# Attention, channel mixing and expert layer in one kernel: PSUM banks shared across two stages, mixing products placed inside the second products, and the conversion of the third weights started a chunk later

## The chip, the core and the metric

The kernel runs as one program on one of the eight cores of a Trainium2 chip. The metric is the device time of one execution in microseconds (us). The core's engines run side by side, each with a queue that it takes in order: TensorE (PE, matrix products into PSUM; PEld is its weight load), VectorE (DVE), ScalarE (ACT), GpSimd (POOL) and SyncE (SP, which here only issues DMAs). PSUM has eight banks of 128 x 512 fp32; a matrix product writes into one bank, and a bank is used again only after its last reader.

## The reference

```python
scores = scale * q @ k.T + bias          # 2 batches, 8 heads, 768 x 768, head dim 64; 8 global and 96 local keys kept
x = softmax(scores) @ v                  # -> x (2, 768, 512)
u = x + (x^T @ U @ V)^T                  # mixing over the sequence, rank 32
x = u + relu(u @ w_ch1) @ w_ch2          # channel sums, hidden 2048
logits = x @ w_gate; local_gate = sigmoid(x @ w_local)
e = argmax(logits) where s == 0 or local_gate < 0.5, else the e of the token before
out = p[e] * (relu(x @ w1[e]) @ w2[e])   # 8 experts, hidden 1024
```

Inputs are fp32, except U, V, w_ch1 and w_ch2, which come as 64-bit floats and are converted on the chip.

## The kernel before, in words

The order of work on each engine is written out by hand: the program order of the instructions is the order of each queue, and generators stepped between other work place the small pieces. A product of two fp32 operands is three products of halves (`three`: high x high, high x low, low x high); a high half is a copy by ACT, the low half a subtraction by DVE or POOL that reads it.

*Attention* runs over 16 heads and 6 tiles of 128 rows. Between its steps the first conversions of weights go along: `load_w1` issues the loads of 64-bit weights on SP, and `from_f64` (lines 217 to 224) turns a piece of 128 x 512 into fp32 with one ACT and four DVE instructions. `load_pair` and `load_v` put the heads' inputs on the same SP queue.

*Channel sums.* `chunks(b, ...)` goes over 16 chunks of 128 hidden channels, batch 0 and then batch 1. In each, `gemm1` makes two halves of 384 tokens, each 12 products into a bank g of two; ACT and DVE make hh and hl of them. `gemm2` of the chunk before then goes over six token tiles, three products each, into the six sums y. Beside it run: `convert(p + 2)`, one step per half and per tile (16 steps, then a load of the weights after next); `split_w1` (`prep`), which gives high halves to ACT and low halves to POOL (line 244, two pieces per pair of chunks); and a `Weave`, ticked once per half and per tile, which for batch 0 steps `mixing(1)`. That sums t1 over six tiles of batch 1 (line 483; its high and low parts come from lines 489 and 487), waits MXW ticks, and then makes six products mx (line 499) into banks of g, each added to x by DVE (line 500), MXS ticks apart. After the chunks, the last few `gemm2` go tile by tile, and `tail` adds each finished sum to x (line 647), stores it (line 648, on SP), and for batch 1 hands it to `routing`, stepped by `late` inside what follows: transposes xt, logits lp (line 717), the choice on DVE (lines 723 to 767), sums over tokens (ab, line 754), slots (sl, line 771), and lists written by POOL.

*PSUM.* In this stage the pool psc holds six banks acc (t1 of batch 1 and the sums y), and psg two for everything else (g). At the end of batch 1 psc is closed, and pools psz (four acc, the experts' sums z) and pss (two side tiles, for `late`) are opened over the same banks.

*Experts.* Two fillers of 128 tokens (positions -2 and -1) come first, while the router finishes; then eight positions of one or two tiles. `unit` takes two chunks of hidden channels of an expert. With one tile it makes egr, which ACT turns into eh (line 1208); the next unit transposes it (`turn_`, etr; hh by ACT on line 1216, hl by DVE on line 1217), and `out_` makes the six products into z. `after` ticks `late` and steps the splits of coming expert weights (line 834 on ACT, line 837 on DVE). `filler_load` issues those weights on SP (line 817).

Of the kernel before, what the change touches and what calls it, by code (L numbers as in the profile page):

```python
# [9 lines left out]
F32 = mybir.dt.float32  # L10
# [9 lines left out]
PSUM = bass.MemoryType.PSUM  # L20
DRAM = bass.MemoryType.DRAM

P = 128
# [6 lines left out]
NP1 = FC1 // 2  # L30
FC2 = 8
NP2 = FC2 // 2
# [37 lines left out]
def tile_kernel(ctx, tc, q, k, v, nn, U, V, w12, wg, wgt, ew, masks, lst0, out, dbg=None):  # L70
    nc = tc.nc
# [10 lines left out]
    def g_tile(name):  # L82
        return g_pool[-1].tile([P, 512], F32, tag="g", name=name)
# [7 lines left out]
    def drain(gen):  # L91
        while gen is not None and run(gen):
            pass
# [152 lines left out]
    def convert(p):  # L246
        w_f[p] = wf0_tile(f"wf{p}") if p < 2 else wf_tile(f"wf{p}")
        for c in range(2):
            raw = w_raw.pop((p, c))
            for h in (0, 512):  # L250
                yield from from_f64(w_f[p][:, c, h:h + 512], sq_w, raw[:, h:h + 512])
            if p + 1 < NP1:
                load_w1(p + 1, c)
# [216 lines left out]
    def mixing(b):  # L470

        if b == 0:
            ut_tiles(0)
            parts = [[t.rearrange("p k c -> p (k c)")[:, DM * i:DM * i + DM] for t in ut[0]] for i in range(NT)]
        else:
            parts = [[mix_room[i % 2][:, w, DM * (i // 2 % 2):DM * (i // 2 % 2) + DM] for w in range(2)] for i in range(NT)]
        t1 = (g_tile if b == 0 else acc_tile)(f"t1_{b}")
        lag = LAGM[b]
        for i in range(NT + lag):
            j = i - lag  # L480
            if j >= 0:
                for w in range(2):
                    nc.tensor.matmul(
                        t1, u_sb[:, j].rearrange("p a r -> p (a r)"), parts[j][w], start=(j == 0 and w == 0), stop=(j == NT - 1 and w == 1))
            if 0 < i <= NT:
                hi, lo = parts[i - 1]
                (nc.gpsimd if (i - 1) % 4 in LOP[b] else nc.vector).tensor_tensor(lo, x_t[b, i - 1], hi.bitcast(F32), ALU.subtract)
            if i < NT:
                nc.scalar.copy(parts[i][0], x_t[b, i])
            yield  # L490
        tm = utp.tile([P, DM], F32R, tag="tm", name=f"tm_{b}")
        nc.scalar.copy(tm, t1)
        yield
        nc.vector.tensor_tensor(tm[32:64], t1[32:64], tm[32:64].bitcast(F32), ALU.subtract)
        for _ in range(MXW if b else 1):
            yield
        for i in range(NT):
            mx = g_tile(f"mx{b}{i}")
            nc.tensor.matmul(mx, vst[:, P * i:P * i + P], tm, start=True, stop=True)
            nc.vector.tensor_tensor(x_t[b, i], mx, x_t[b, i], ALU.add)  # L500
            for _ in range(MXS if b else 1):
                yield
# [25 lines left out]
    for z in range(total + LAGV):  # L528
        if z < total:
            n, i = steps[z]  # L530
            zz = z % (2 * NT)
            if zz == LAGV and n // 2 + 1 < len(heads) // 2:
                load_v(n // 2 + 1)
            if n == 2 and i == 0:
                load_w1(0, 0)
                load_w1(0, 1)
            if i == 1 and 0 < n + 1 < H:
                head_bias(n + 1)
            if zz == 1 and n > 1 and n // 2 + 1 < len(heads) // 2:
                load_pair(n // 2 + 1)  # L540
            s = scores(z)
        if z >= LAGT and z - LAGT < total:
            transposed(z - LAGT)
        if z < total:
            softmax(z, s)
        if z == 0:
            other_columns()
        if z >= LAGV:
            values(z - LAGV)
        if z == 2 * NT:  # L550
            flagi = banded_form()
        if z == half - 1:
            banded.append(nc.values_load(flagi[0:1, 0:1], min_val=0, max_val=1))
        if z == half + LAGV:
            drain(mixc)
            t_ctx.close()
            other_windows(0)
            if "x" in dbg:
                for i_ in range(NT):
                    nc.sync.dma_start(dbg['x'][0, P * i_:P * i_ + P, :], x_t[0, i_])  # L560
            utp = u_ctx.enter_context(tc.tile_pool(name="ut", bufs=1, side="right"))
            fill = [mixing(0), transposes(0)]
        if z > half + LAGV and z % FILL[1] < FILL[0] and fill and not run(fill[0]):
            fill.pop(0)
        if z == MZ:
            run(mixc)
        if z > SM0:
            run(small)
        if z > BG0:
            if z % 8 < BGR and bg and not run(bg[0]):  # L570
                bg.pop(0)
# [13 lines left out]
    sm = ctx.enter_context(tc.tile_pool(name="small", bufs=2))  # L585
    m_ctx = ExitStack()
    mp = m_ctx.enter_context(tc.tile_pool(name="moe1", bufs=3))
    c_ctx = ExitStack()
    psc = [c_ctx.enter_context(tc.tile_pool(name="psc", bufs=1, space=PSUM))]

    def acc_tile(name):
        return psc[0].tile([P, 512], F32, tag="acc", bufs=6 if len(psc) == 1 else 4, name=name)

    def side_tile(name):

        return g_tile(name) if len(psc) == 1 else psc[1].tile([P, 512], F32, tag="side", bufs=2, name=name)

    def three(out_, ah, al, bh, bl, start, stop):
        nc.tensor.matmul(out_, ah, bh, start=start, stop=False)
        nc.tensor.matmul(out_, ah, bl, start=False, stop=False)  # L600
        nc.tensor.matmul(out_, al, bh, start=False, stop=stop)  # L601
# [347 lines left out]
    acc = {}  # L949
# [11 lines left out]
    def chunks(b, weave, hook, tail):  # L961

        conv, prep = None, None
        for m in range(FC1):
            p = m // 2
            if m % 2 == 0:
                drain(prep)
                prep = None
                if b == 0 and p + 2 < NP1:
                    drain(conv)  # L970
                    conv = convert(p + 2)
            hook(m)
            if m == 0 or m != 1 and m % 2 == 1 - b:
                if p + 1 < NP1:
                    prep = split_w1(b, p + 1)
                elif b == 0:
                    drain(conv)
                    prep = split_w1(1, 0)
            for _ in gemm1(b, m):
                run(prep, 1)  # L980
                run(conv, 1)
                if b == 1:
                    split_step(2)
                weave.tick()
                if b == 0 and m < 2:
                    weave.tick()
            if m == 0:
                acc[b] = []
            elif m <= FC1 - DEFER[b]:
                for i in range(NT):  # L990
                    if m == 1:
                        acc[b].append(acc_tile(f"y{b}{i}"))
                    gemm2(b, m - 1, i, acc[b])
                    run(conv, 1)
                    if b == 1 and i % 2:
                        split_step()
                    weave.tick()
        weave.finish()
        if prep is not None:
            drain(prep)  # L1000
        hook(FC1)
        for i in range(NT):
            for m in range(FC1 - DEFER[b], FC1):
                gemm2(b, m, i, acc[b])
                if b == 1:
                    late.tick()
            tail(i)
# [52 lines left out]
    chunks(1, wv, fillers_ahead, tail1)  # L1060
    while splits:
        split_until(99)
    c_ctx.close()
    psc[:] = [ctx.enter_context(tc.tile_pool(name=n, bufs=1, space=PSUM)) for n in ("psz", "pss")]
    filler_load(0, 1)
    filler_load(0, 3)

# [106 lines left out]
    def after(step):  # L1174
        late.tick()
        if step:
            split_step()
# [17 lines left out]
    def unit(pos, p, key, xh, xl, n, acc_):  # L1195

        wh, wl = e_hl[key, p]
        if n == 1:
            g = g_tile(f"eg{key}{p}")
            gv = g[:, :256].rearrange("p (a c) -> p a c", a=2)  # L1200
            for kk in range(KC):
                s_ = slice(P * kk, P * kk + P)
# [6 lines left out]
            hh = ep.tile([P, 256], F32R, tag="ehh", bufs=3, name=f"ehh{key}{p}")  # L1209
            hl = ep.tile([P, 256], F32R, tag="ehl", bufs=3, name=f"ehl{key}{p}")  # L1210
# [6 lines left out]
                nc.vector.tensor_tensor(hl, tr[:, :256], hh.bitcast(F32), ALU.subtract)  # L1217

            def out_():
                for c in range(2):  # L1220
                    s_ = slice(P * c, P * c + P)
                    f = 2 * p + c
                    three(acc_[0], hh[:, s_], hl[:, s_], wh[:, c, 512:], wl[:, c, 512:], f == 0, f == FC2 - 1)
                    after("cd"[c] in PACE[pos])
                if p == NP2 - 1:
                    done(pos)

# [11 lines left out]
        else:  # L1239
            for c in range(2):  # L1240
                f = 2 * p + c
# [3 lines left out]
                hh, hl = e_gemm1(key, f, WIDTHS[pos], xh, xl, turn, [end[0][:, w, 256 * (f % 4):256 * (f % 4) + 256] for w in range(2)] if late_f else None)  # L1245
# [92 lines left out]
_OUTS = [((NTOK, DM), "float32")]  # L1338


MXW, MXS = 26, 4
DEFER = (3, 4)
LAGM = 3, 3
SPM = 12, 13, 14
# [101 lines left out]
```

## Time and profile before

| | us |
|---|---|
| three runs | 611.58, 614.37, 614.12 (median 614.12) |
| the profiled execution | 612.27, its span 610.4, mean granted clock 0.989 |
| PE busy | 585.3 (96%) |
| DVE busy | 415.6 (68%) |
| ACT busy | 292.7 (48%) |
| POOL busy | 127.3 (21%) |

The span goes from the first instruction to the last, and the run's time is a little longer. Busy PE counts the modelled time of products that overlap, so PE's gaps and the granted clock say more than its share. Attention takes the span to about 114 us, the chunks of batch 0 to about 252, those of batch 1 to about 411, and fillers and experts the rest. Times in the rows below are in us from the span's start; the arrow in a bracket names what ended the idle time.

### The profile page before, as it was taken

To read this page: it belongs to the slowest core of one execution; us is meant where nothing else is said; L and a number is where in the kernel's file an instruction comes from. 1 tells how busy PE (TensorE), PEld (TensorE's weight loads), DVE (VectorE), ACT (ScalarE), POOL (GpSimd) and SP (SyncE) were. 2 spreads that over 40 slices of the span, in tenths; PEclk is the share of its full clock that TensorE was granted. 3 is DMA by queue.
4 is the path that set the end of the run, shared out by engine and by line. 5 is a ranking of instruction groups with operands and counts; after the bars stand their busy time and mean duration, and the time that the engine had idled before them with its cause. 6 is when DMAs were issued, how large, how long until landed. Compare 5 with 4: busy or idle time off the path is not lost. (4 is left out here: it accounts for less than half of the span.)

```text
span 610.4 us, 9735 instructions
## 1 busy us (share of the span) xinstructions
PE 585.3 (96%) x3469; PEld 519.3 (85%) x3469; DVE 415.6 (68%) x998; ACT 292.7 (48%) x631; POOL 127.3 (21%) x119
## 2 busy tenths in 40 slices
PE   8999999889989999999998999998899999999994
PEld 5998899879878999899997889877788988989893
DVE  5779986498888881348999446566724577685850
ACT  4878877534413432332222116324524677584841
POOL 5010030112213333333330211012230313031101
PEclk9999999899999999999999999997999999999998
DMA  8956651014414300251000038035096578868400
GB/s 215 310 153 202 209 171 49 2 45 162 139 69 139 111 27 1 90 187 35 35 18 0 1 62 319 35 121 155 20 319 247 178 272 319 267 247 319 168 15 35
DMA packets 35850, 83.47 MB, mean 137 GB/s; under 512 B 5631, under 2 KB 17791, under 8 KB 33744
## 3 DMA queue, kind: packets, MB, share of 16 engines
q1 hardware_dynamic: 31632, 70.87, 35.1%
q0 software_dynamic: 2784, 7.62, 3.5%
q10 hardware_dynamic: 1376, 4.26, 1.8%
q8 instruction: 29, 0.48, 0.4%
q14 instruction: 29, 0.24, 0.1%
HBM read 74.34 MB, written 8.77 MB: 136 GB/s over the span
## 5 line engine op out<-in xcount | busy, mean ns | idle before, releaser
L604 ACT ACTIVATE hh<-g 128x384 fp32r<-128x384 f32 x62 | 30.4, 490 | 112.0 <-PE g L601 111.6
L605 DVE SCALAR_TENSOR_TENSOR hl<-g,hh 128x384 fp32r<-128x384 f32 x62 | 34.4, 556 | 52.3 <-ACT hh L604 52.1
L338 PE MATMUL s<-kt,q 128*128 128x232 f32 (+1 forms) x192 | 55.2, 370 | 2.6 <-DVE m L348 1.7
L352 ACT ACTIVATE e<-t,m 128x232 f32<-128x232 f32 (+1 forms) x96 | 45.7, 477 | 17.2 <-DVE m L348 16.7
L672 DVE CUSTOM_DVE_ANT_0 sq_w<-x,wgt 128x512 f32<-128x512 f32 x54 | 47.1, 872 | 1.4
L348 DVE CUSTOM_DVE_ANT_0 t<-s,bias 128x232 f32<-128x232 f32 (+1 forms) x96 | 35.9, 377 | 16.6 <-PE s L338 6.8
L217 ACT ACTIVATE sq_w<-w 128x512 f32<-128x512 f32 x32 | 21.5, 671 | 49.6 <-DVE wf L224 49.6
L859 POOL DMA_INDIRECT out_dram<-x,ids x13 | 13.2, 1013 | 120.6 <-ACT x L858 100.0
L365 ACT COPY et<-pt 128x256 f32<-128x256 f32 (+1 forms) x96 | 33.5, 349 | 6.7 <-PE pt L362 4.7
L362 PE MATMUL pt<-ident,e 128*128 128x128 f32 x176 | 35.0, 273 | 0.0
L338 PEld LDWEIGHTS s<-kt,q 128*128 128x128 f32 x192 | 29.7, 191 | 5.9 <-DVE m L348 3.9
L222 DVE SCALAR_TENSOR_TENSOR wf<-w,wf 128x512 int32<-128x512 int32 x32 | 32.5, 1017 | 0.8
L382 PE MATMUL o<-v,et 128*128 128x65 f32 x160 | 30.9, 275 | 0.0
L780 POOL DMA_INDIRECT lst<-tab,slot x12 | 12.7, 1054 | 81.0 <-DVE tab L776 80.0
L605 DVE SCALAR_TENSOR_TENSOR ehlr<-egr,ehhr 128x192 fp32r<-128x192 f32 (+1 forms) x28 | 10.6, 377 | 26.1 <-ACT ehhr L604 26.1
L220 DVE SCALAR_TENSOR_TENSOR wf<-w,wf 128x512 int32<-128x512 int32 x32 | 27.1, 848 | 1.1 <-DVEq L463 0.7
L362 PEld LDWEIGHTS pt<-ident,e 128*128 128x128 f32 x176 | 24.1, 142 | 4.3 <-ACT et L365 0.5
L381 PE MATMUL o<-v,et 104*128 104x65 f32 x160 | 26.9, 249 | 0.0
L381 PEld LDWEIGHTS o<-v,et 104*128 104x128 f32 x160 | 24.2, 191 | 0.8
L382 PEld LDWEIGHTS o<-v,et 128*128 128x128 f32 x160 | 24.3, 191 | 0.0
L604 ACT ACTIVATE ehhr<-egr 128x192 fp32r<-128x192 f32 (+1 forms) x28 | 9.7, 347 | 29.1 <-PE egr L601 27.6
L224 DVE SCALAR_TENSOR_TENSOR wf<-sq_w,wf 128x512 f32<-128x512 f32 x32 | 22.0, 688 | 1.3
(753 smaller groups left out, 1943.5 us busy)
## 6 DMA issues: line engine op xcount, KB each, us to landing
ew<-in_ew_dram SPq DMA_DIRECT2D x32, 1024.0 KB, 6.8
w<-in_w_dram SPq DMA_DIRECT2D x16, 1024.0 KB, 4.9
v<-in_v_dram SPq DMA_DIRECT2D x8, 704.0 KB, 5.1
ew<-in_ew_dram ACTq DMA_DIRECT2D x4, 1024.0 KB, 12.9
x2d<-x SPq DMA_DIRECT2D x12, 256.0 KB, 2.0
kt<-in_k_dram SPq DMA_DIRECT2D x7, 408.0 KB, 4.5
q<-in_q_dram SPq DMA_DIRECT2D x14, 192.0 KB, 5.5
wgt<-in_wgt_dram SPq DMA_DIRECT2D x4, 512.0 KB, 4.8
```

Of the source, the lines that this page charges most:

```text
L220: nc.vector.scalar_tensor_tensor(t, low, 29, t, ALU.logical_shift_right, ALU.bitwise_or)
L222: nc.vector.scalar_tensor_tensor(t, high, -0x40000000, t, ALU.bitwise_and, ALU.bitwise_or)
L338: nc.tensor.matmul(s[:, :w], qs[n % 2][:, c], kt[:, kc], start=True, stop=True)
L348: nc.vector.tensor_tensor_reduce(out=t[:, :w], in0=s[:, :w], in1=bias[:, h, b0:b0 + w], scale=-0.125, scalar=3.0e38, op0=ALU.add, op1=ALU. ...
L352: nc.scalar.activation(e[:, :w], t[:, :w], AF.Exp, bias=m, scale=-1.0)
L362: nc.tensor.transpose(pt[:, P * j:P * j + P], e[:, c0:c0 + P], ident)
L365: nc.scalar.copy(et[:, :w], pt[:, :w])
L381: nc.tensor.matmul(oo, et[0:REST, 0:P], vt[0:REST, NT + i - 1, vc], start=True, stop=False)
L382: nc.tensor.matmul(oo, et[:, P:256], vt[:, i, vc], start=False, stop=True)
L604: nc.scalar.activation(hi, src, AF.Relu)
L605: nc.vector.scalar_tensor_tensor(lo, src, 0.0, hi.bitcast(F32), ALU.max, ALU.subtract)
L672: nc.vector.tensor_tensor_reduce(out=sq_w, in0=x_t[0, i], in1=rooms[k % 2][:, DM * j:DM * j + DM], scale=1.0, scalar=0.0, op0=ALU.mult, op ...
```

## The change

The pool psc stays open to the end, with four banks acc and two banks side. t1 of batch 1 and the last two sums of each batch use side, the first four acc; the experts' sums go on in acc, and the side tiles of `late` in side, after `beside` is set. `convert(p + 2)` is drained and started at odd chunks and no longer at even ones. MXW and MXS become 31 and 8. In `out_` with one tile, the products that read hl come behind the four others. `load_w1(0, ...)` is called two steps later in attention.

```diff
--- before.py
+++ after.py
@@ -474,7 +474,7 @@
             parts = [[t.rearrange("p k c -> p (k c)")[:, DM * i:DM * i + DM] for t in ut[0]] for i in range(NT)]
         else:
             parts = [[mix_room[i % 2][:, w, DM * (i // 2 % 2):DM * (i // 2 % 2) + DM] for w in range(2)] for i in range(NT)]
-        t1 = (g_tile if b == 0 else acc_tile)(f"t1_{b}")
+        t1 = (g_tile if b == 0 else two_tile)(f"t1_{b}")
         lag = LAGM[b]
         for i in range(NT + lag):
             j = i - lag
@@ -531,7 +531,7 @@
             zz = z % (2 * NT)
             if zz == LAGV and n // 2 + 1 < len(heads) // 2:
                 load_v(n // 2 + 1)
-            if n == 2 and i == 0:
+            if n == 2 and i == 2:
                 load_w1(0, 0)
                 load_w1(0, 1)
             if i == 1 and 0 < n + 1 < H:
@@ -585,15 +585,18 @@
     sm = ctx.enter_context(tc.tile_pool(name="small", bufs=2))
     m_ctx = ExitStack()
     mp = m_ctx.enter_context(tc.tile_pool(name="moe1", bufs=3))
-    c_ctx = ExitStack()
-    psc = [c_ctx.enter_context(tc.tile_pool(name="psc", bufs=1, space=PSUM))]
+    psc = ctx.enter_context(tc.tile_pool(name="psc", bufs=1, space=PSUM))
+    beside = []
 
     def acc_tile(name):
-        return psc[0].tile([P, 512], F32, tag="acc", bufs=6 if len(psc) == 1 else 4, name=name)
+        return psc.tile([P, 512], F32, tag="acc", bufs=4, name=name)
+
+    def two_tile(name):
+
+        return psc.tile([P, 512], F32, tag="side", bufs=2, name=name)
 
     def side_tile(name):
-
-        return g_tile(name) if len(psc) == 1 else psc[1].tile([P, 512], F32, tag="side", bufs=2, name=name)
+        return (two_tile if beside else g_tile)(name)
 
     def three(out_, ah, al, bh, bl, start, stop):
         nc.tensor.matmul(out_, ah, bh, start=start, stop=False)
@@ -966,9 +969,9 @@
             if m % 2 == 0:
                 drain(prep)
                 prep = None
-                if b == 0 and p + 2 < NP1:
-                    drain(conv)
-                    conv = convert(p + 2)
+            elif b == 0 and p + 2 < NP1:
+                drain(conv)
+                conv = convert(p + 2)
             hook(m)
             if m == 0 or m != 1 and m % 2 == 1 - b:
                 if p + 1 < NP1:
@@ -989,7 +992,7 @@
             elif m <= FC1 - DEFER[b]:
                 for i in range(NT):
                     if m == 1:
-                        acc[b].append(acc_tile(f"y{b}{i}"))
+                        acc[b].append((acc_tile if i < 4 else two_tile)(f"y{b}{i}"))
                     gemm2(b, m - 1, i, acc[b])
                     run(conv, 1)
                     if b == 1 and i % 2:
@@ -1060,8 +1063,7 @@
     chunks(1, wv, fillers_ahead, tail1)
     while splits:
         split_until(99)
-    c_ctx.close()
-    psc[:] = [ctx.enter_context(tc.tile_pool(name=n, bufs=1, space=PSUM)) for n in ("psz", "pss")]
+    beside.append(True)
     filler_load(0, 1)
     filler_load(0, 3)
 
@@ -1217,11 +1219,13 @@
                 nc.vector.tensor_tensor(hl, tr[:, :256], hh.bitcast(F32), ALU.subtract)
 
             def out_():
+                parts = [slice(P * c, P * c + P) for c in range(2)]
                 for c in range(2):
-                    s_ = slice(P * c, P * c + P)
-                    f = 2 * p + c
-                    three(acc_[0], hh[:, s_], hl[:, s_], wh[:, c, 512:], wl[:, c, 512:], f == 0, f == FC2 - 1)
+                    nc.tensor.matmul(acc_[0], hh[:, parts[c]], wh[:, c, 512:], start=(p == 0 and c == 0), stop=False)
+                    nc.tensor.matmul(acc_[0], hh[:, parts[c]], wl[:, c, 512:], start=False, stop=False)
                     after("cd"[c] in PACE[pos])
+                for c in range(2):
+                    nc.tensor.matmul(acc_[0], hl[:, parts[c]], wh[:, c, 512:], start=False, stop=(p == NP2 - 1 and c == 1))
                 if p == NP2 - 1:
                     done(pos)
 
@@ -1338,7 +1342,7 @@
 _OUTS = [((NTOK, DM), "float32")]
 
 
-MXW, MXS = 26, 4
+MXW, MXS = 31, 8
 DEFER = (3, 4)
 LAGM = 3, 3
 SPM = 12, 13, 14
```

## Rows read from the trace of the kernel before

**Rows 1.** The page's busy time by engine, whole span.
```profile
PE 585.3 (96%) x3469; PEld 519.3 (85%) x3469; DVE 415.6 (68%) x998; ACT 292.7 (48%) x631; POOL 127.3 (21%) x119
```

**Rows 2.** Waits of PE, whole span: us in total, times, longest.
```profile
PE t L483 <- DVE mix_room L487: 2.7, 3, 1.4
...
PE g L599 <- DVE x L500: 1.6, 2, 1.1
PE lp L717 <- DVE x L647: 1.6, 1, 1.6
```

**Rows 3.** Stretches: length, busy us by engine, granted clock, DMA share, GB/s.
```profile
414.20:422.60 8.40, 8.40 (x40) 7.21 (x41) 4.99 (x23) 3.54 (x9) 2.47 (x4) 0.59 0.87 241
422.60:438.00 15.40, 13.21 (x84) 10.51 (x83) 13.91 (x48) 9.21 (x21) 2.52 (x4) 1.00 0.08 24
414.00:421.00 7.00, 6.83 (x35) 6.06 (x36) 3.52 (x19) 2.64 (x7) 2.47 (x4) 0.62 0.81 194
...
114.80:118.40 3.60, 3.58 (x12) 3.60 (x13) 0.00 (x0) 0.00 (x0) 0.00 (x0) 0.57 0.03 7
```

**Rows 4.** DVE in order of time, chunks 0 and 1: start, duration, instruction.
```profile
121.31 1.90 DVE L487 TENSOR_TENSOR mix_room<-x,mix_room 128x512 fp32r<-128x512 f32 x1 [1.11 <-ACT mix_room L489]
...
123.60 2.55 DVE L220 SCALAR_TENSOR_TENSOR wf<-w,wf 128x512 int32<-128x512 int32 x1
126.07 1.28 DVE L487 TENSOR_TENSOR mix_room<-x,mix_room 128x512 fp32r<-128x512 f32 x2
```

**Rows 5.** POOL in order of time, chunk 0.
```profile
120.29 2.37 POOL L244 TENSOR_TENSOR w01l<-wf,w01h 128x1024 fp32r<-128x1024 f32 x1 [31.55 <-ACT w01h L243]
123.20 2.40 POOL L244 TENSOR_TENSOR w01l<-wf,w01h 128x1024 fp32r<-128x1024 f32 x1 [0.54 <-ACT w01h L243]
```

**Rows 6.** PE in order of time, chunk 1; in brackets the idle time before.
```profile
126.80 1.10 PE L483 MATMUL t<-mix_room,u_sb 128*128 128x512 f32 x3 [0.72 <-DVE mix_room L487]
```

**Rows 7.** DVE in order of time, chunk 5.
```profile
168.10 2.78 DVE L222 SCALAR_TENSOR_TENSOR wf<-w,wf 128x512 int32<-128x512 int32 x1
170.81 0.68 DVE L500 TENSOR_TENSOR x<-mx,x 128x512 f32<-128x512 f32 x1
171.41 0.68 DVE L224 SCALAR_TENSOR_TENSOR wf<-sq_w,wf 128x512 f32<-128x512 f32 x1
```

**Rows 8.** PE in order of time, the two halves of gemm1 in chunk 6.
```profile
171.63 0.41 PE L599 MATMUL g<-uth,w03h 128*128 128x384 f32 x1 [1.07 <-DVE x L500]
...
174.53 0.44 PE L599 MATMUL g<-uth,w03h 128*128 128x384 f32 x1 [0.57 <-DVE x L500]
```

**Rows 9.** DVE in order of time, around the passage to the fillers.
```profile
405.72 0.69 DVE L647 TENSOR_TENSOR x<-y,x 128x512 f32<-128x512 f32 x1 [0.89 <-PE y L601]
...
415.24 0.17 DVE L723 TENSOR_REDUCE nm<-lp 128x1 f32<-128x8 f32 x1 [1.21 <-PE lp L717]
...
417.21 0.16 DVE L773 CAST slot<-sl 128x2 int32<-128x2 f32 x1 [0.66 <-PE sl L771]
...
419.62 0.42 DVE L1217 TENSOR_TENSOR ehlr-20_4589<-etr-20_4612,ehhr-20_4588 128x256 fp32r<-128x256 f32 x1 [1.36 <-ACT ehhr-20_4588 L1216]
```

**Rows 10.** PE in order of time, end of the first filler.
```profile
436.84 0.50 PE L601 MATMUL z-20_4547<-ehr-2_3_4229,ehlr-23_4764 128*128 128x512 f32 x1 [1.39 <-DVE ehlr-23_4764 L1217]
...
437.87 0.28 PE L599 MATMUL egr-11_4891<-er-1_1h,xfh 128*128 128x256 f32 x1
```

**Rows 11.** ACT in order of time, first filler.
```profile
423.43 1.14 ACT L834 CAST er-1_1h<-ew 128x512 fp32r<-128x512 f32 x2
425.08 0.37 ACT L1216 CAST ehhr-21_4639<-etr-21_4676 128x256 fp32r<-128x256 f32 x1 [0.51 <-PE etr-21_4676 L1215]
```

**Rows 12.** SP's issues in order of time, two places.
```profile
14.85 0.85 SPq L239 DMA_DIRECT2D w<-in_w_dram  x2
...
414.64 1.04 SPq L817 DMA_DIRECT2D ew<-in_ew_dram  x2
```

**Rows 13.** The raw weights w, one line: durations ns min/median/max, first and last start.
```profile
L220 DVE SCALAR_TENSOR_TENSOR wf<-w,wf x32: 681/692/2550, 43.9 to 225.5; 128x512 int32<-128x512 int32 x32
```

## The prediction

> **What bounds the kernel now.** First the page's busy time: PE works 585.3 of 610.4 us [rows 1], so only its gaps and its slow stretches are for sale. Second, the waits of PE, longest first [rows 2]: three that the diff touches are the channel sum t1 of the second batch waiting for DVE (2.7 us in three waits), the first products g waiting for the addition of a mixing product (1.6 in two), and the router's logits lp waiting 1.6 for an addition of line 647. [...] Last, from 422.6 to 438.0 DVE is busy 13.91 of 15.4 us and PE 13.21 [rows 3]: there DVE sets the pace, and PE's waits for it are a consequence.
>
> **The change part by part.** The sum is made against the profiled execution, 612.27 us (span 610.4 and 1.87 around it).
>
> *Conversion of the third weights a chunk later.* In chunk 0 the conversion's L218, L220 and ACT's square stand between the splits of the second batch's rows (L487). It is not less work: two steps leave chunk 0's gemm1, six more that were drained in one go at the head of chunk 2 are spread, and each load of raw weights that follows a conversion is issued a chunk later; two raw buffers and one whole chunk between a load and its reader are as in the later pairs of before. What goes first: L220 at 123.60 took 2.55 us against a median of 0.69 [rows 4, 13], ended 0.55 us after POOL's split of 123.20 to 125.60 [rows 5], and only then came the next two L487 at 126.07 [rows 4], for which t1 waited 0.72 at 126.80 [rows 6]. Without L220 that L487 starts at 123.6, itself ends about 0.6 after POOL's split, which starts some 0.5 earlier, so near 125.7, and the following one near 126.3: t1's three products follow about 1.0 earlier. The first wait (1.4) doesn't shrink: L487 of 121.31 ended 123.21, 0.55 after POOL's first split (120.29 and 2.37) [rows 4, 5], and started earlier it would still end there. The last L487 keeps one conversion step in front of it, as now. I take 0.9 us; ends: 0 (POOL holds the new order up as well) and 3.2 (all waits of t1 in rows 2, and 0.5 for ACT's part).
>
> The rows show a DVE operation with two SBUF inputs ending 0.55 us after POOL's, however early it began. [...]
>
> *Mixing products inside the second products.* The six products mx stood at chunks 4 to 7, at the first or fifth tile of gemm2, two in some chunks; they now come one per chunk, 5 to 10, behind the second tile. mx takes one of the two banks of g, so g of the next chunk waits for the addition L500. Before, the addition of chunk 5's first mx stood behind L222, which POOL stretched to 2.78 us, and came at 170.81 [rows 7]; g waited 1.07 at 171.63 and 0.57 at 174.53 [rows 8]. With one mx per chunk the first g of the next chunk takes the bank that no mx used, and the second, one half of gemm1 later (2.3 us by the two starts less the wait, rows 8), takes mx's. The addition now stands behind L224 as well: 171.4 and 0.68, done at 172.1 [rows 7]; PE would ask at about 172.3. In chunk 5 it just fits; in 7 and 9, where no second mx has slowed PE, I allow 0.2 of wait each. With the restart after each gap, the two old waits cost 2.2 (1.07, 0.57 and about 0.3 of refilled pipeline each), so 1.8 is saved. Ends: 2.2, and a loss (a rival below).
>
> *Banks passed on.* The experts' banks were new pools laid over the old one, and lp, first tile in them, waited for the last reader of the whole pool, the sixth tile's addition on line 647 [rows 2]. Now lp takes the bank of the fifth tile's sum, added at 405.72 [rows 9]. So lp goes when PE gets there, 1.6 us earlier, and the drop of the clock has no cause. [...] But DVE is next: its gaps of 1.21 (lp), 0.66 (sl) and 1.36 (transposes by a slow PE) [rows 9] go, 3.2 us. Then a transfer is late: SP issues the next weights only behind the sixth tile's store, at 414.64 [rows 12], which doesn't move. The queue moved 194 GB/s from 414 to 421, 1.36 MB [rows 3]; the 0.26 MB of the store and the first 1.05 MB of weights are through at 421.0. The cast that reads them was at 423.43 [rows 11]: 2.4 earlier, no more. ACT's next cast (ehhr-21) had 0.51 idle before it [rows 11] and comes 2.9 earlier, and behind that DVE is full to 438, so all follows by 2.9.
>
> *The order within out_.* The two products that read hl go last, behind four that don't. After the last wait (1.39 at 436.84) PE still had four products, 1.03 us to 437.87 [rows 10]; now two: 0.5 less. In the later one-tile experts PE shows no such wait, so nothing there. The work hung on between the products comes one or two products earlier, behind the same DVE operations: nothing. Stage: 2.9 and 0.5 less 0.1 for such waits, 3.3 us. Ends: 1.1 (the weights land only at 423.4: 0.6 from ACT's idle time, and 0.5) and 5.2 (no transfer in the way: 3.2, and the 1.5 that DVE is idle from 422.6 to 438, and 0.5).
>
> *First weights loaded two steps later.* Two loads move past load_pair(2) on SP's queue (three transfers that wait for PE); they were issued at 14.85 [rows 12], and the first reader is at 43.9 [rows 13]. Nothing; if that cover were gone, DVE would wait ahead of the scores' softmax. load_v behind them was held by PE anyway.
>
> Sum: 0.9, 1.8 and 3.3 are 6.0: 606.3 for this execution. The three runs have a median of 614.12 and a mean of 613.4, 1.1 above it; I put the forecast by the mean, 607.4.
>
> **Rivals**, all from 613.4. (a) The weights land late: stage 3 gives 1.1, total 3.8, 609.6. For it: two loads share the queue. Against: the bytes of rows 3. (b) The half clock comes back elsewhere. PE will still wait for DVE after 422, 1 to 2 us in a piece, and waits of that length were followed by the lower level at 114.8 and 414 [rows 3], but the one of 1.39 at 436.84 by none; 3.4 us are lost again: 2.6 gained, 610.8. [...] (c) It doesn't do what it says: the first side tile gets the sixth tile's bank in the rotation, lp waits as before, and the stage gives only 0.5: 3.2, 610.2. (d) Slower: the additions. In chunks 5, 7 and 9 the addition stands behind two stretched conversions and L224; if DVE runs a further 1.1 us late there (as the wait of rows 8), g waits each time, and the clock falls each time, for between 1.5 (the 3.6 us of rows 3) and 3.4: three times 3.6 is 10.8 lost against 0.9, 2.2 and 3.3 gained, 617.8. It decides from about 0.5 us of lateness on; DVE has spare time in even chunks, which speaks against it. (e) DVE and the transfer give more than drawn: 8 in all, 605.4.
>
> **How the numbers follow.** Chances: forecast 0.50, (a) 0.17, (b) 0.13, (c) 0.07, (d) 0.06, (e) 0.07. 0.5%, 3.1 us, is about what a measurement can tell here (the runs before spread over 2.8). Faster by more: the forecast but for a small part, (a) in the main, (e), half of (c): 0.75. Within: (b) and the rest, 0.19. Slower: 0.06. The range takes in (e)'s edge and most of (b): 604.3 to 611.4; the forecast's own is 606 to 609.
>
> **What would show it.** lp starts with no wait and nm on DVE follows the sixth addition at once; the granted clock stays 1.00 from 412 to 424; ACT's cast of er-1_1h starts at a landing, near 421, no longer behind its own work; the waits of g for L500 are gone and one t1 wait is shorter. Wrong if lp still waits for line 647, if g waits for L500 in odd chunks, or if the clock drops in another place.

## The result, and the profile after

The changed kernel took 606.50 us (median of 4 runs, 605.48 to 607.19), the kernel before 613.01 in 4 runs beside it (611.58 to 614.37): a ratio of 0.9901, 95% interval 0.9874 to 0.9927. Forecast were 607.4, and 604.3 to 611.4. The profiled execution of after took 607.19 us with a span of 605.3, that of before 612.27 with 610.4.

The page of after, busy time by engine. PE has 3.3 us less of it than in [rows 1] for the same 3469 instructions: the same products, at a higher mean clock (0.993, before 0.989).

```profile
PE 582.0 (96%) x3469; PEld 518.1 (86%) x3469; DVE 416.8 (69%) x998; ACT 292.0 (48%) x631; POOL 128.1 (21%) x119
```

PE's waits in after (us in total, times, longest). Against [rows 2] the one for lp is gone, that of g for L500 is at 0.2, but t still waits 2.5 in two pieces, and a wait for a gather, gt, has come in.

```profile
PE t L483 <- DVE mix_room L487: 2.5, 2, 2.0
PE ab L757 <- DVE ab L742: 1.9, 2, 1.0
PE gt L810 <- DMA x<-x2d,idc: 1.9, 1, 1.9
PE z-20_4540 L1228 <- DVE ehlr-23_4757 L1219: 1.7, 1, 1.7
...
PE g L602 <- DVE x L500: 0.2, 1, 0.2
```

Stretches of after; columns as in [rows 3], the clock is the third figure from the end. The first two are the passage: full clock, where before had 8.4 us at 0.59. In the third, DVE is about as full as before (13.27 of 15 us; 13.91 of 15.4). The last is a stretch near half clock in chunk 1, behind t's wait of 2.0; before had one of 0.57 in chunk 0, 8 us earlier [rows 3].

```profile
407.00:412.00 5.00, 5.00 (x37) 3.97 (x35) 3.81 (x13) 1.10 (x4) 0.00 (x0) 1.00 0.06 20
412.00:420.00 8.00, 7.75 (x54) 6.61 (x55) 6.78 (x28) 5.29 (x13) 3.63 (x6) 1.00 0.90 293
420.00:435.00 15.00, 12.36 (x76) 9.86 (x75) 13.27 (x48) 8.66 (x20) 3.01 (x5) 1.00 0.08 21
122.40:126.50 4.10, 4.10 (x15) 3.82 (x14) 3.13 (x4) 1.25 (x3) 1.26 (x1) 0.58 0.00 0
```

Where the 5.1 us of span went, by the start of the same product in both profiles: 0.3 is there at the first product of the first layer (before 114.82, after 114.51), 1.4 at chunk 2's (136.16, 134.78), 2.5 at chunk 14's (239.73, 237.26) and so still at the first filler's (411.62, 409.14), 6.3 at the first product of the second filler's second unit (437.87, 431.54), 5.0 at the product behind the transposes of position 1's gathered rows (460.44, 455.41) and to the end. So 0.3 came ahead of all edits but the later loads in attention, 1.07 in chunks 0 and 1, 1.10 from the mixing products, 3.85 in the passage, and 1.3 was lost again. The later loads were not run alone; the first product of the first layer starts at 113.73 to 115.37 in the seven profiles below without them and at 113.50 to 114.96 in the seven with them, so the 0.3 is not theirs as far as this shows.

### The profile page after: what moved, and what is told of

Its sections match the earlier page's. It is cut to its first block, busy times and chain, and to the rows that moved or that the text cites. A ratio compares the mean times of both kernels' runs of the same rounds, so it can differ in the third digit from the quotient of the medians.

```text
span 605.3 us, 9730 instructions
## 1 busy us (share of the span) xinstructions
PE 582.0 (96%) x3469; PEld 518.1 (86%) x3469; DVE 416.8 (69%) x998; ACT 292.0 (48%) x631; POOL 128.1 (21%) x119
## 5 line engine op out<-in xcount | busy, mean ns | idle before, releaser
L222 DVE SCALAR_TENSOR_TENSOR wf<-w,wf 128x512 int32<-128x512 int32 x32 | 32.5, 1017 | 0.8
L220 DVE SCALAR_TENSOR_TENSOR wf<-w,wf 128x512 int32<-128x512 int32 x32 | 25.6, 800 | 1.1 <-DVEq L463 0.7
L224 DVE SCALAR_TENSOR_TENSOR wf<-sq_w,wf 128x512 f32<-128x512 f32 x32 | 22.1, 691 | 1.7
```

The costliest lines, as they stand in the source:

```text
L220: nc.vector.scalar_tensor_tensor(t, low, 29, t, ALU.logical_shift_right, ALU.bitwise_or)
L222: nc.vector.scalar_tensor_tensor(t, high, -0x40000000, t, ALU.bitwise_and, ALU.bitwise_or)
```

## The experiments

Each kernel below was timed in 5 rounds against before, four kernels to a chip (after: the runs above). The table has, of each profile, four stretches between the starts of the same products, in us: A, from chunk 0 to chunk 2 (g of w00h to g of w01h), with the lowest granted clock of a 4 us slice in it; B, chunks 4 to 14 (w02h to w07h), where the mixing products lie; C, the passage (egr-20 to egr-11), with the lowest clock of a 5 us slice; D, from position 0's first product into z to the product behind the transposes gt of position 1's gathered rows (egr-14). "Equal clock" is explained below it.

| kernel | median us | ratio, 95% | A, clock | B | C, clock | D | against before at equal clock |
|---|---|---|---|---|---|---|---|
| before | 610.6 to 613.0 | | 21.34, .57 | 86.97 | 26.25, .56 | 8.02 | 0 |
| after | 606.50 | .9874–.9927 | 20.27, .63 | 85.87 | 22.40, 1.00 | 9.33 | −4.5 ± 0.8 |
| after again | 606.95 | .9893–.9957 | 20.31, .64 | 85.84 | 21.40, 1.00 | 9.59 | −4.5 ± 0.6 |
| conversion | 611.78 | .9957–1.0 | 20.29, .57 | 86.95 | 27.84, .50 | 9.28 | −0.6 ± 0.5 |
| mixing | 610.89 | .9949–.9996 | 21.45, .60 | 85.86 | 24.75, .66 | 9.06 | −1.3 ± 0.5 |
| conversion, mixing | 609.58 | .9934–.9976 | 19.14, 1.00 | 85.89 | 23.58, 1.00 | 9.26 | −1.9 ± 0.5 |
| banks | 608.47 | .9902–.9954 | 21.34, .67 | 86.96 | 22.90, 1.00 | 9.10 | −1.9 ± 0.7 |
| out_ order | 610.24 | .9951–.9991 | 19.88, 1.00 | 86.96 | 25.79, .50 | 8.04 | −1.6 ± 0.5 |
| before, early gather | 609.63 | .9915–.9963 | 19.88, 1.00 | 86.95 | 26.30, .50 | 7.23 | −2.5 ± 0.7 |
| after, early gather | 604.44 | .9848–.9915 | 19.11, 1.00 | 85.87 | 22.60, .66 | 7.23 | −6.2 ± 0.7 |
| after, mx at first tile | 606.83 | .9899–.9957 | 20.29, .57 | 86.23 | 22.16, 1.00 | 9.10 | −3.8 ± 0.6 |
| after, split later | 607.35 | .9913–.9963 | 22.20, .60 | 85.87 | 21.70, 1.00 | 9.24 | −3.5 ± 0.6 |
| after, early weights | 606.04 | .9870–.9909 | 20.29, .62 | 85.84 | 21.40, 1.00 | 8.85 | −4.3 ± 0.7 |
| after, both early | 603.77 | .9821–.9866 | 20.62, .73 | 85.85 | 21.42, 1.00 | 7.24 | −6.3 ± 0.8 |

Runs of one kernel differ by their granted clock: 65 runs of before lie at 609.1 to 610.9 where their mean clock was 0.994 and at 614.0 to 615.7 where it was 0.986. A straight line of time against clock, one slope for all kernels (466 us for 1.00, ± 50) and an offset for each kernel, leaves 0.8 us of scatter; the offsets are the last column. What an edit does to the clock is not in it: before had a mean clock of 0.9902, the banks alone 0.9947, after 0.9932.

**The banks alone** (fixed banks from the channel sums to the experts in place of two new pools; the two places of the edit that matter most):

```diff
-    c_ctx.close()
-    psc[:] = [ctx.enter_context(tc.tile_pool(name=n, bufs=1, space=PSUM)) for n in ("psz", "pss")]
+    beside.append(True)
```

> The kernel before with only the shared PSUM pool (four acc, two side banks, never closed). Theory: lp no longer waits 1.6 us for line 647, the half clock after it goes, and DVE's three gaps close until ACT's cast of er-1_1h waits for its weights; 3.4 us at the passage, less up to 1.3 at the gather of position 1: 609.6 to 610.9 against 613.0, lp without a wait, granted clock 1.00 from 412 to 424. Rival, that the clock's phase made the gain and not the wait: the wait goes but the clock drops at another place, under 1 us gained. Rival, that the order within out_ made the gain: under 1 us.

608.47, against 612.95 for before on the same chip: about 4.4 us (2.8 to 6.0 by the interval), more than expected and the largest part. Of the 3.4 expected at the passage, which C confirms (26.25 less 22.90), up to 1.3 had been taken off for a loss at the gather that is not this edit's, as the early gather on before shows below. In the table, 1.9 of the gain stands at equal clock; the mean clock, 0.0045 higher, makes another 2.1 by the slope. One row of the passage in before and one with the banks alone, at the same times, show it:

```profile
415.00:420.00 5.00, 5.00 (x24) 4.20 (x24) 2.56 (x16) 2.29 (x7) 2.00 (x3) 0.56 0.91 180
```

```profile
415.00:420.00 5.00, 5.00 (x36) 4.40 (x36) 4.23 (x14) 2.74 (x7) 2.40 (x5) 1.00 0.98 315
```

PE is busy for all 5 us in both, but gets 36 products done in place of 24.

**The order in out_ alone** (the added lines in part):

```diff
+                for c in range(2):
+                    nc.tensor.matmul(acc_[0], hl[:, parts[c]], wh[:, c, 512:], start=False, stop=(p == NP2 - 1 and c == 1))
```

> The kernel before with only the new order of the six products in out_. Theory: only the last wait for ehlr counts, 0.5 us less (two products more stand in front of it), lp wait and half clock as before: 612.5 against 613.0. Rival: both waits for ehlr of before (0.8 and 1.4) vanish, 2.2 us, 610.8.

Stretch C is 0.46 shorter at the same mean clock (0.87 in both), the 0.5 forecast. Of the rival's two waits the first (0.8) is gone, but the last reads 1.7 in place of 1.4, with its product at 25.2 us into C in both, and two products behind it in place of four: so the rival's mechanism falls. By time, though, 610.24 is the rival's number: 1.6 ± 0.5 at equal clock, about 1.1 more than C shows. A is shorter by 1.46 there, but with the old code and at full clock, as in another kernel with the old code; D is 8.04, some 1.1 under most, but after has the same order and 9.33. The difference stays open.

**The mixing products alone:**

```diff
-MXW, MXS = 26, 4
+MXW, MXS = 31, 8
```

> The kernel before with only MXW, MXS = 31, 8. Theory: chunks 4 to 7 lost 2.6 us over their products to the additions of line 500, and one mx per odd chunk still loses about 0.5 in each of three: 1.1 us gained, 611.9, first t1 waits as before (2.7). Rival, that the places only fit with the conversion a chunk later: no gain, waits of g for line 500 of 1 us and more remain, 613.0.

B falls by 1.11, as in after (1.10), and the time by 1.3 ± 0.5; the rival, that it needs the later conversion, falls.

**The conversion alone:**

```diff
-                if b == 0 and p + 2 < NP1:
-                    drain(conv)
-                    conv = convert(p + 2)
+            elif b == 0 and p + 2 < NP1:
+                drain(conv)
+                conv = convert(p + 2)
```

> The kernel before with only the conversion of the third weights started a chunk later. Theory: one t1 wait of 0.7 goes (the one behind L220), the first t1 wait stays since the row's split ends 0.55 us after POOL's however early it starts (it may even read longer), g's waits for line 500 stay at 1.6: 612.3. Rival, shared bandwidth in place of blocking: the first wait shrinks too, 1.3 gained, 611.7.

A falls by 1.05 with a stretch near half clock in both profiles, the time by 0.6 ± 0.5. The first wait of t reads 2.0 in place of 1.4, against the rival of shared bandwidth.

**Conversion and mixing products together:**

> The kernel before with the later conversion and the later mixing products, and nothing of the banks or the out_ order. Theory: these two are worth 0.5 to 0.9 and 1.1 to 1.3 and add: 1.6 to 2.2 under before, 20.3 (with a stretch at half clock) or 19.1 (without) from the first to the second chunk's first product, 85.87 from the third to the eighth, and the passage keeps its lp wait of 1.6 and a half clock behind it. Rival: they share slack and give 1.2 or less together.

1.9 ± 0.5: they add. Here A ran at full clock, and 19.14 against the 19.88 of two kernels with the old code at full clock is what the edit itself saves, 0.74. This profile also has the lp wait of 1.6, but no drop of the clock behind it: the one of six with that wait. Stretch C in before and here:

```profile
411.62:437.87 26.25, 22.48 (x127) 18.41 (x127) 21.07 (x75) 13.34 (x31) 4.98 (x8) 0.87 0.32 91
```

```profile
408.87:432.45 23.58, 19.58 (x127) 16.04 (x127) 20.81 (x75) 13.24 (x31) 4.99 (x8) 1.00 0.29 102
```

By their mean clock in C the kernels with that wait and the old order in out_ stand in line: 23.58 at 1.00, 24.75 at 0.93, 26.25 and 26.30 at 0.87, 27.84 at 0.82.

**After again**, unchanged:

> The kernel after, unchanged, as the base for its variants, and a second profile of it. Theory: the times of before spread with the granted clock, and the waits that the change removed are removed in every execution, so here too lp has no wait, the clock is 1.00 from 410 to 422, the g waits for L500 are at 0.2 or less, and the time is 605.5 to 607.2 (ratio 0.988 to 0.992). Theory on position 1's gather: its wait of 1.9 is chance, not the change's (the kernels with the conversion alone and with the mixing products alone show 1.6 to 1.8 as well), so it may be 0.6 or 1.9 here. Rival: the earlier passage causes it, then 1.6 to 2.0 again.

PE's waits are the same but for two transfers: the one for the gather is 2.1 (D 9.59), which by itself suits the rival as well and is decided by the early gather on before; and the weights that ACT's cast in the passage waits for came 1.1 earlier, C being 1.0 shorter.

**The early gather on after**:

```diff
-                if pos + 1 < E:
+                if 0 < pos < E - 1:
                     gathered(pos + 1)
...
                 late.finish()
+                gathered(1)
```

> Changes when position 1's rows are gathered: they are asked for right after position 0's lists, ahead of the next store, instead of behind it. Theory: PE's wait for this gather (0.6 to 1.9 in seven profiles) goes, z to the next position's first product takes about 7.5 us instead of 8.0 to 9.3, and the time is 0.6 to 1.9 under the kernel after's. Rival: the DMA engines are full from 440 to 456 (share 0.95 or more), so the early gather only pushes the weights of position 1 back, and PE waits for those instead: no gain, or up to 1 us worse.

604.44 against 606.95 for after on the same chip, and D at 7.23: the wait is gone, the rival (weights late in its stead) refuted. This is the wait in after: POOL's issues, first the store and then the first of the gather's two; ACT's weight loads, three just ahead of it and a fourth just behind; and PE's product.

```profile
444.59 1.04 POOL L862 DMA_INDIRECT out_dram<-x,fl_idx  x1 [7.46 <-ACT x L861]
446.19 1.06 POOL L803 DMA_INDIRECT x<-x2d,idc  x1 [0.28 <-POOL idc L800]
```

```profile
443.77 1.66 ACTq L820 DMA_DIRECT2D ew<-in_ew_dram  x3
446.43 0.38 ACTq L820 DMA_DIRECT2D ew<-in_ew_dram  x1
```

```profile
455.00 0.66 PE L810 MATMUL gt<-ident,x 128*128 128x128 f32 x4 [1.88 <-DMA x<-x2d,idc]
```

The gather is issued at 446.19 behind a store that waited for ACT, and its first rows are there only near 455, 8.8 us later. From 440 to 455 the DMA share, the last figure but one, was 0.99:

```profile
440.00:455.00 15.00, 13.10 (x85) 11.18 (x83) 3.24 (x7) 3.45 (x8) 4.81 (x7) 1.00 0.99 384
```

**The same early gather on before:**

> The kernel before with nothing changed but the early gather of position 1's rows. Theory (the wait for this gather is no consequence of the change, it stands in before with the same size in most executions): 1.2 to 2.2 under before, and z to the next product 7.2 to 7.5 instead of 8.0 to 9.3. Rival (the earlier passage of the change makes the gather late): 0.6 or less under before.

−2.5 ± 0.7 at equal clock, and D at 7.23, with no wait ahead of gt:

```profile
457.29 0.60 PE L807 MATMUL gt<-ident,x 128*128 128x128 f32 x4
```

On the 8.02 of before's own profile this would be worth 0.8; the 2.5 says that most executions of before wait longer than that one. So the wait stands in before as well, and the 1.3 us that after lost between the two profiles is not a consequence of the change: D is 8.85 to 9.59 in nine of the eleven profiles without the early gather, also in those with the passage of before, and 8.0 in two, of which before's is one. The expectation's theory holds; the reading that a shorter passage makes the gather late falls.

**The mixing products at the first tile:**

```diff
-MXW, MXS = 31, 8
+MXW, MXS = 30, 8
```

> The kernel after with the mixing products at the first tile of the second products of a chunk instead of the second. Theory: what is left of the mixing products' loss, 0.48 us in each of chunks 6, 8 and 10, is the wait for the addition at L500 behind a 2.78 us operation of VectorE at L222; an earlier addition goes ahead of that one and takes the three losses away: the stretch from the third to the eighth chunk of weights' first products falls from 85.87 to 84.4 to 84.8, the time by 1.0 to 1.4. Rival: VectorE has no free place there either and the loss moves to the tile that waits for the operation at L222: 85.5 to 86.5, no gain.

The rival held: B is 86.23, worse than 85.87. L500 goes ahead of L224 but not of L222, and so only from 169.91 to 169.50 in a profile that runs 0.3 later; g no longer waits for it, but mx itself now waits 0.3 until DVE has read the bank that it takes, three times (PE's waits):

```profile
PE mx L499 <- DVE hl L608: 0.9, 3, 0.3
```

**The split a chunk later:**

```diff
-            if m == 0 or m != 1 and m % 2 == 1 - b:
+            if m % 2 == 1 - b:
```

> The kernel after with the first halves of the second weights' split of w1 (one conversion of chunk 0) a chunk later. Theory: TensorE's wait for t in chunk 0, 1.98 us, is for VectorE's and GpSimd's conversions ahead of it; with one less the wait falls to about 0.9, and the stretch at half clock that follows it (granted 0.63 from 123 to 127) shrinks or goes: 1.1 by the wait alone, up to 2.2 with the clock, 20.27 to 18.1 to 19.2 from the first to the second chunk's first product. Rival: the conversion moved is late in chunk 1 and TensorE waits there: no gain, 20.0 to 20.6.

The rival held here too, and A is worse than it said (22.20). PE waits in chunk 1 instead:

```profile
126.94 0.49 PE L483 MATMUL t<-mix_room,u_sb 128*128 128x512 f32 x1 [1.22 <-DVE mix_room L487]
130.33 0.50 PE L483 MATMUL t<-mix_room,u_sb 128*128 128x512 f32 x1 [1.90 <-DVE mix_room L487]
```

and a stretch near half clock stands behind that wait (131 to 135, where after has 1.00), beside one of 0.74 from 115 to 119:

```profile
131.00:135.00 4.00, 4.00 (x12) 3.15 (x11) 3.70 (x6) 1.13 (x2) 0.00 (x0) 0.60 0.00 0
```

**The weights of the passage asked for earlier:**

```diff
     def tail1(i):
+        if i == NT - 1:
+            filler_load(0, 1)
         second_input(1, i)
...
-    filler_load(0, 1)
     filler_load(0, 3)
```

> The kernel after with the second weights of the next expert asked for ahead of the last x2d store on SyncE's queue instead of behind it. Theory: ScalarE's wait of 1.0 to 2.1 for these weights in the passage (er-1_1h's cast) goes, and TensorE's 1.7 for ehlr-23 with it in part: the stretch from egr-20 to egr-10 is 16.3 instead of 16.4 to 17.4, the time 0 to 1 under the kernel after's. Rival: the transfer takes the place of the x2d store in the DMA engines and the rows gathered later come late: 0.5 to 1 slower.

ACT's cast has no wait left (2.14 in after, 1.00 in after again), and C is 21.40: no shorter than in after again. PE still waits 1.7 for ehlr-23. So with the weights there, DVE sets the pace, as drawn, and the edit only takes out up to 1 us of an execution's bad luck. At equal clock it shows nothing (−4.3 ± 0.7 against −4.5 ± 0.6). Without the edit the landing sets C: in after, mx at the first tile, split later and early gather the cast starts 9.08, 8.85, 8.38 and 9.25 us into C, and C ends 13.3 behind it each time; from 7.92 on down it stays at 21.40.

**Both early:**

> The early gather and the earlier weights together on the kernel after. Theory: the gather's gain of 1.6 to 2.5 and the weights' 0 to 1 stand in different stretches and add: 603.4 to 604.6. Rival: the gather now meets the same transfers and waits as before, or the earlier weights cost something: 604.6 to 606.

603.77 us, 0.9843 of before, interval 0.9821 to 0.9866: the fastest measured, and faster than both kernels of the case. How much of it the weights give beside the gather is not settled (604.44 on another chip; −6.3 and −6.2 at equal clock).

## Why the prediction was right

*Passage, forecast 3.3 us: 3.85 between the two profiles; mechanism right, but most of the gain is the clock.* The products and the reduction stand as drawn: lp (PE) starts without a wait, and nm follows the sixth addition at once.

```profile
409.95 1.03 PE L720 MATMUL lp<-wg_sb,x 128*128 128x9 f32 x8
```

```profile
410.87 0.67 DVE L650 TENSOR_TENSOR x<-y,x 128x512 f32<-128x512 f32 x1
411.46 0.16 DVE L726 TENSOR_REDUCE nm<-lp 128x1 f32<-128x8 f32 x1
```

The 1.21 ahead of nm in [rows 9] is gone. The transfer was drawn to be through at 421.0 on before's time; ACT's cast started at a landing, at 418.21, which is 420.69 there:

```profile
418.21 1.14 ACT L837 CAST er-1_1h<-ew 128x512 fp32r<-128x512 f32 x2 [2.14 <-DMA ew<-in_ew_dram]
```

The split of the term wasn't drawn, and the runs give it. At full clock C is 23.58 with the lp wait and 22.90 with the banks passed on: 0.7 (the cast waits 1.96 for its weights there; with them earlier, by the 1.0 of after again, the estimate is up to 1.7). The order in out_ is 0.5: PE's last two products in after come behind the wait, where [rows 10] had four:

```profile
430.96 0.74 PE L1228 MATMUL z-20_4540<-ehr-2_3_4229,ehlr-23_4757 128*128 128x512 f32 x2 [1.71 <-DVE ehlr-23_4757 L1219]
```

The other 2.7 (26.25 less 23.58) is the half clock behind the lp wait, and that differs by execution: C was 24.75 to 27.84 in the five profiles that had it.

*Mixing products, forecast 1.8: 1.1, the mis-sized term.* The old loss was taken at 2.2 and what is left at two waits of 0.2. With 16.60 for a pair of chunks without mixing products (w06h to w07h, the same in both kernels) and 0.23 for each of the six products, B of before is 86.97 − 83.0 − 1.4 = 2.6 over, and after 1.5. The remainder was the larger miss: a third wait, behind chunk 5, was taken as none, and the 0.3 counted beside each of the old waits was left out beside the new ones. DVE's order came as forecast in kind, but with L222 at 2.78 and L224 ahead of the addition in all three odd chunks 5, 7 and 9:

```profile
166.48 2.78 DVE L222 SCALAR_TENSOR_TENSOR wf<-w,wf 128x512 int32<-128x512 int32 x1
169.30 0.69 DVE L224 SCALAR_TENSOR_TENSOR wf<-sq_w,wf 128x512 f32<-128x512 f32 x1
169.91 0.68 DVE L500 TENSOR_TENSOR x<-mx,x 128x512 f32<-128x512 f32 x1
```

L500 ends at 170.59 and g starts at 170.65, after 0.15 idle; behind chunk 5 it did not just fit. Of the third one the trace has the releaser:

```profile
205.76 0.44 PE L602 MATMUL g<-uth,w05h 128*128 128x384 f32 x1 [0.16 <-DVE x L500]
```

Three such gaps are the 1.5: 0.49 each, of which 0.15 is idle time. Of the other 0.33 or so PE's starts show most: the products come 0.17 to 0.18 apart, but the one ahead of the gap, the one behind it and the next start at 170.16, 170.65 and 170.93, in all 0.42 later than at that pace, 0.27 of it beside the idle time. In before the gap at 174.53 has 0.27 beside its idle time too (starts at 173.62, 174.53 and 174.81), close to the 0.3 of the forecast; that this is a refilled pipeline is the prediction's reading, which no run shows. The slower rival (d) needed longer waits and a falling clock; neither came (0.15 each, and 1.00 from 151.39 to 237.26).

*Conversion, forecast 0.9: 0.74 at full clock; mechanism right, the size a little off.* "The first wait (1.4) doesn't shrink": it even reads 1.98, but nothing is lost by that. Compare the order of out_ alone (old code) with conversion and mixing together, both at full clock in A, where the first product of w00h starts at 114.27 and 115.37. L487 starts 0.55 earlier behind that product in the second, and ends 6.92 behind it in both, 0.55 after POOL's first piece; the product that waits starts 6.97 behind it in both. DVE in the one and the other:

```profile
119.30 1.89 DVE L487 TENSOR_TENSOR mix_room<-x,mix_room 128x512 fp32r<-128x512 f32 x1 [1.11 <-ACT mix_room L489]
```

```profile
119.85 2.44 DVE L487 TENSOR_TENSOR mix_room<-x,mix_room 128x512 fp32r<-128x512 f32 x1 [0.89 <-ACT mix_room L489]
```

The wait reads longer because PE gets there 0.55 earlier: its wait for ACT's copy (L489) just before, 0.63, is down to 0.08. What is saved is the later wait of 0.72 [rows 6], which is gone with L220. The forecast of 1.0 for it let POOL's second piece end as much earlier as it starts; it starts 0.55 earlier but takes 2.80 where [rows 5] had 2.40. In after, DVE, POOL (both pieces, then the second by itself) and PE:

```profile
118.98 2.44 DVE L487 TENSOR_TENSOR mix_room<-x,mix_room 128x512 fp32r<-128x512 f32 x1 [0.90 <-ACT mix_room L489]
```

```profile
118.50 5.16 POOL L244 TENSOR_TENSOR w01l<-wf,w01h 128x1024 fp32r<-128x1024 f32 x2 [30.09 <-ACT w01h L243]
120.86 2.80 POOL L244 TENSOR_TENSOR w01l<-wf,w01h 128x1024 fp32r<-128x1024 f32 x1
```

```profile
121.47 0.50 PE L483 MATMUL t<-mix_room,u_sb 128*128 128x512 f32 x1 [1.98 <-DVE mix_room L487]
```

By the rows (2.55, 2.78, 2.44 and 1.90, each ending 0.55 after a piece of POOL's) DVE's duration is set by POOL's end: in both profiles the median of L220, L222 and mix_room's L487 is 0.68 to 0.69. What holds DVE up no run takes apart.

*Rivals.* (a), weights late: not in the sense of 423.4; they landed 0.3 ahead of the drawn time, and 1.1 ahead of that in a second execution. (b), half clock elsewhere after 422: in one of the eight profiles with the banks passed on (after with the early gather, 0.66 from 420 to 425), not in the others. The 3.4 of (b) and (d) is an estimate from [rows 3], 8.40 us times the 0.41 that 0.59 is short of full clock (the clock read 0.50 from 416 to 422). In that one profile it cost nothing like it: C is 22.60, what the landing of its weights alone gives; that fits DVE setting the pace in that place. (c) fell with lp's start.

*Two of its signs of being wrong came, in small.* g does wait for L500 behind the odd chunks, 0.15 each. And the clock drops in another place: the stretch of 0.57 behind the idle time at 114.8 [rows 3] is gone in after, and one of 0.58 stands behind t's wait of 1.98, from 122.4 on. Of the eight profiles with that wait it comes in five (0.57 to 0.64), and not in conversion and mixing together and after with the early gather (no drop in A), nor with both early, where one stands at 115 as in before (0.73). Two with the old conversion have none in A either. The drop costs 1.2 there and 1.5 in the old place (20.27 less 19.11, 21.34 less 19.88), so the profiles of before and after owe 0.3 of A's 1.07 to it.

*The sum.* 6.0 were forecast from profile to profile and 5.1 came: 0.5 more up to chunk 2 (0.3 ahead of chunk 0, and the half clock in A), 0.7 less from the mixing products, 0.5 more from the passage, and 1.3 lost to a gather which in the profile of before came early by chance. With that chance apart it is 6.4, near the 6.5 between the medians. The mechanisms came as drawn, but that the sum is this close is in part luck, since the misses of 0.5 and 0.7 cancel. The gains at equal clock of the banks, the order in out_, and conversion with mixing, 1.9, 1.6 and 1.9, make 5.4 against 4.5 ± 0.8 for after: within the intervals, with the part in out_ as the one whose gain no trace explains. The prediction put the forecast 1.1 above the profile's own time because the profiled execution was a lucky one; that step was right, and the gather is one of the places where its luck was.

## What to carry to other kernels

A new pool laid over an old one made its first tile wait for the last reader of all of it, 1.6 us here; passing the banks on by name took that wait away. A wait of 1.6 us on TensorE cost 2.7 us more by the clock behind it, and since that differs by execution, a small edit is to be read from stretches at equal clock, not from two spans. A wait that reads longer (1.98 for 1.4) need not cost more: look at when the product behind it starts. Before a late transfer is put down to a change, look for it in other executions of the kernel before.

## What the runs showed of the hardware

That the half clock behind one and the same wait comes in most executions but not in all (0.50 to 0.66 behind the lp wait in five profiles, 1.00 in one) was not expected, nor that the 6 us by which runs of one kernel differ go for the most part with the mean granted clock (0.8 us of scatter are left). Why the same wait is followed by half clock in one execution and not in another stays open. The second surprise is the gather: issued behind weight loads with the DMA engines at a share of 0.99, its first rows took 8.8 us, and asking 10 us earlier (436.27 in the last kernel, with the first product at 451.69 and no wait) removed the whole wait and brought PE no new one.
